# The last three attention units and the routing of the last five token tiles, written out by hand

## The chip, the cores and the metric

One NeuronCore of one Trainium2 chip runs one program. The metric is the device time of one execution in microseconds (us), as the median of several runs. The engines are TensorE (PE, its weight loads PEld), VectorE (DVE), ScalarE (ACT), GpSimd (POOL) and SyncE (SP, which issues most DMAs).

## The reference, cut to what matters

```python
x = _attn_ref(q, k, v)          # 2 x 8 heads, 576 tokens, head size 64; heads 0-3 local mask (32), 4-7 strided mask
x = x.transpose(0, 2, 1, 3).reshape(1152, 512)
x = _moe_ref(x, w_gate, w1, w2, capacity)     # top-1 of 8 experts
return _moe2_ref(x, w_in, w_out, a, b)        # rational activation between two products

# _moe_ref
logits = x @ w_gate
expert_idx = np.argmax(logits, axis=1)
gate_w = softmax(logits)[np.arange(N), expert_idx]
# token i takes the next place of its expert, if there is one below capacity
h = np.maximum(np.einsum('ecd,edf->ecf', disp, w1), 0.0)
y = np.einsum('ecf,efd->ecd', h, w2)
out[i] = gate_w[i] * y[expert_idx[i], pos[i]]  # 0 for tokens without a place
```

All arithmetic is float32 in effect; the products of the expert stage are float32 matmuls.

## The kernel before, in words

The program has three stages. The first is attention, in 16 units (u0 to u15). A unit is one batch, one pair of heads and half of their query blocks. Each unit passes through steps that a software pipeline spreads over four turns of a loop: `stage_a` (scores on PE: a mask product and then queries by keys), `stage_exp` (row maximum on DVE, exponentials on ACT), `stage_norm` (sum and reciprocal on DVE, then the scaling of the two heads' weights, both halves on POOL), `stage_b` (transposes on PE into a PSUM tile `tp` for each head), `stage_copy` (`tp` to `pT`, head 0 on DVE for these units and head 1 on ACT), `stage_c` (weights by values on PE, into `pv`) and `stage_evac` (`pv` into the 512 x 1152 array `xT` on DVE). Units 12 to 15 fill the first two of xT's four rows of 128 features for the second batch; a unit covers 288 tokens.

The routing needs, for each tile of 128 tokens (nine tiles, 0 to 8): `gate_mm`, the logits, from four products (d = 0 to 3, one for each 128 features); `gate_arg`, nine small DVE steps and one on ACT that find the expert and the gate weight; `rows_mm` and `put_rows`, which transpose the tile's rows back, scale them by the gate and write them to the DRAM array `xd`; `rank_mm` and `rank_post`, which count each token's place in its expert and build one-hot rows `ohr` on DVE; and `index_mm`, which turns the one-hots into token numbers. `places` sorts the experts by their count, `index` writes the lists `idx` for the gathers (128 entries and up to 64 more for each expert), `ordi` is the order of the experts (SP needs it to load their weights), and `over` computes `flag`, which says whether any expert needs the long way round.

In the loop the tiles 0 to 3 are routed in turns 9 to 15, out of a list `dq` of small steps; `hook(14, rank(0, 4))` puts the ranking of tiles 0 to 3 into turn 14. Three extra turns (`LE = 3`) then drain the pipeline: no new unit starts, and gates, rows and ranks of tiles 4 and 5 are put between the last steps. Tiles 6 to 8 follow behind the loop.

Each engine takes its instructions in the order in which the program lists them, so the order written here is the order on each engine. All waits between engines are semaphores.

Then the memory pools of attention are closed and those of the second stage opened over the same memory. `gather(0)` issues two indirect DMAs on POOL (expert 0's 192 rows out of `xd`), `warm(16)` runs 16 dummy matmuls on PE, SP starts two weight loads, all engines read `flag` and take the branch over the long way, `warm(12)` runs 12 more dummy matmuls, and `xpose(0)` transposes the gathered rows. The expert stage follows: eight experts, each four weight tiles of the first product (line 912 of the profile) and four of the second (line 927); weights stream in on SP. The third stage is the dense product with the rational activation.

The lines that the steps below speak of: 325 and 329 scores, 352 to 355 softmax, 363 to 366 normalising, 375 transposes, 383 copies, 393 values, 401 into xT, 423 logits, 457 rows, 463 and 465 scaled rows, 480 and 483 rank, 494 one-hots, 513 index products, 551 to 554 index lists, 697 gathers, 281 dummy matmuls, 712 and 713 transposes of the gathered rows, 854 and 855 flag and branch.

Of the kernel before, what the change touches and what calls it, by code (L numbers as in the profile page):

```python
# [19 lines left out]
T = B * S  # L20
# [18 lines left out]
NL = 64  # L39
DUM2 = (16, 12)  # L40
LE = 3
# [98 lines left out]
def build(tc, qt, kt, vv, masks, cb, cf, wl, cap, wf, ab, out):  # L140
# [227 lines left out]
    def stage_b(u):  # L368
        s_ = st[u]
        nb, Q, KN = geom(*u[1:])[:3]  # L370
        s_["tp"] = []
        for h in range(2):
# [3 lines left out]
            s_["tp"].append(tp)  # L376

    def stage_copy(u, h):
        s_ = st[u]
        nb, Q, KN = geom(*u[1:])[:3]  # L380
        if h == 0:
            s_["pT"] = att.tile([128, 2, 3, 128], F32, name="pT", bufs=2)[0:KN, :, 0:nb, 0:Q]
        (A.copy if h or u[1:] in ((2, 1), (3, 1)) else V.tensor_copy)(out=s_["pT"][:, h], in_=s_["tp"][h])

# [132 lines left out]
    kc, key, pos, wide, offe = (rt.tile([128, E], F32, name=x) for x in ("kc", "key", "pos", "wide", "offe"))  # L517
    gtm, pm, m8 = (rt.tile([128, E, E], F32, name=x) for x in ("gtm", "pm", "m8"))
    ordi = rt.tile([128, E], I32, name="ordi")

    def bc(x, axis, n=E):
        return x.unsqueeze(axis).to_broadcast([128, n, E] if axis == 1 else [128, E, n])

    def places(total):

        return [
            lambda: V.tensor_scalar(out=kc, in0=total, scalar1=capf, scalar2=None, op0=ALU.min),
            lambda: V.scalar_tensor_tensor(out=key, in0=kc, scalar=float(E), in1=cft[:, F_PRIO:F_PRIO + E], op0=ALU.mult, op1=ALU.add),
            lambda: V.tensor_tensor(out=gtm, in0=bc(key, 1), in1=bc(key, 2), op=ALU.is_gt),
            lambda: V.tensor_reduce(out=pos, in_=gtm, axis=AX.X, op=ALU.add),  # L530
            lambda: V.tensor_tensor(out=pm, in0=bc(cft[:, F_IOTA:F_IOTA + E], 2), in1=bc(pos, 1), op=ALU.is_equal),
        ]
# [6 lines left out]
    def by_expert(out, x):  # L539

        V.tensor_tensor(out=m8, in0=pm.rearrange("p s e -> p e s"), in1=bc(x, 1), op=ALU.mult)
        V.tensor_reduce(out=out, in_=m8, axis=AX.X, op=ALU.add)

    def index():

        ip = late()[0][:, 0:4 * E].rearrange("p (h a e) -> p h a e", h=2, a=2)
        im = att.tile([128, 2, E, 2 * E], F32, name="im", bufs=1)
        ib = att.tile([128, 2, E], F32, name="ib", bufs=1)
        idx = rt.tile([128, 2, E], I32, name="idx")
        for h in range(2):  # L550
            V.tensor_tensor(out=im[:, h].rearrange("p s (a e) -> p s a e", a=2), in0=pm.unsqueeze(2).to_broadcast([128, E, 2, E]),
                            in1=ip[:, h].unsqueeze(1).to_broadcast([128, E, 2, E]), op=ALU.mult)
            V.tensor_reduce(out=ib[:, h], in_=im[:, h], axis=AX.X, op=ALU.add)
            V.tensor_scalar(out=idx[:, h], in0=ib[:, h], scalar1=capm[:, h:h + 1], scalar2=float(T), op0=ALU.mult, op1=ALU.add)
        by_place(ordi, cft[:, F_IOTA:F_IOTA + E])
        return idx
# [61 lines left out]
    for i, t in ((11, 0), (12, 1), (13, 2), (14, 3)):  # L618
        hook(i, lambda t=t: row(t))
    hook(14, lambda: rank(0, 4))  # L620
    for i in range(n + LE):
        ua, uc, un, ub = (at(units, i - k) for k in (0, 3, 1, 2))
        if uc:
            stage_copy(uc, 0)
            stage_copy(uc, 1)
        if ua:
            stage_a(ua)
            stage_exp(ua)
        if uc:
            stage_c(uc)  # L630
        if i == n:
            dq.extend([lambda: gate_mm(6, 9, (2, 3), late()[1]), lambda: index_mm(0, 4)])
        if i == n + 1:
            gates(4, 6)
            row(4)
            rank(4, 6)
            row(5)
        if i == n + 2:
            gate_mm(6, 9, (0,), late()[1])
        for f in hooks.pop(i, []):  # L640
            f()
        if un:
            stage_norm(un)
        if i >= n and ub:
            stage_b(ub)
        if i >= n and uc:
            stage_evac(uc)
        dv(2)
        if i < n and ub:
            stage_b(ub)  # L650
        if i < n and uc:
            stage_evac(uc)
        dv(5 if i < n + 2 else 0)
# [64 lines left out]
    idc = rt.tile([128, NT], I32, name="idc")  # L718
    flag = rt.tile([128, 1], I32, name="flag")

    def over():

        by_place(cnt[:, 4:], kc)
        V.tensor_tensor(out=key, in0=cnt[:, 4:], in1=cft[:, F_SEL:F_END], op=ALU.is_gt)
        V.tensor_reduce(out=flag, in_=key, axis=AX.X, op=ALU.max)

# [358 lines left out]
```

## Time and profile before

| | |
|---|---|
| median of 3 runs | 464.94 us (464.47 to 466.04) |
| the profiled execution | 466.55 us, of which the span from first to last instruction is 464.8 us |
| PE busy | 431.6 us, 93% of the span |
| DVE busy | 325.7 us, 70% |
| ACT busy | 241.7 us, 52% |
| POOL busy | 54.9 us, 12% |
| mean granted TensorE clock | 0.952 of full speed |

Full speed is 2.4 GHz; 0.50 in the profile is the lower of the clock's two levels, 1.2 GHz. The attention stage runs from the start to about 65 us, its tail and the routing to about 103 us, the experts from there to about 245 us and the dense product to the end. The profile is one execution, 1.6 us above the median of the runs, so differences are taken within it and then set against the median.

### The profile page before, as it was taken

To read this page: it belongs to the slowest core of one execution; us is meant where nothing else is said; L and a number is where in the kernel's file an instruction comes from. 1 tells how busy PE (TensorE), PEld (TensorE's weight loads), DVE (VectorE), ACT (ScalarE), POOL (GpSimd) and SP (SyncE) were. 2 spreads that over 40 slices of the span, in tenths; PEclk is the share of its full clock that TensorE was granted. 3 is DMA by queue.
4 is the path that set the end of the run, shared out by engine and by line. 5 is a ranking of instruction groups with operands and counts; after the bars stand their busy time and mean duration, and the time that the engine had idled before them with its cause. 6 is when DMAs were issued, how large, how long until landed. Compare 5 with 4: busy or idle time off the path is not lost.

```text
span 464.8 us, 7758 instructions
## 1 busy us (share of the span) xinstructions
PE 431.6 (93%) x2778; PEld 389.4 (84%) x2779; DVE 325.7 (70%) x720; ACT 241.7 (52%) x579; POOL 54.9 (12%) x86
## 2 busy tenths in 40 slices
PE   7899768769999999999999979999989999999994
PEld 4667557649999999999999969988879989899973
DVE  2786642613466554565676999999979999969992
ACT  3785730202031221212224877878868888678881
POOL 3454430110101011010000000000020000110002
PEclk9999985659999999999999989999999999999998
DMA  8999660339975767878784000000010000010001
GB/s 294 341 357 356 221 233 2 114 129 381 417 299 173 261 212 222 258 236 285 268 291 147 1 1 0 1 0 0 2 68 1 0 1 1 23 47 1 1 1 68
DMA packets 20986, 66.42 MB, mean 143 GB/s; under 512 B 2824, under 2 KB 3208, under 8 KB 20944
## 3 DMA queue, kind: packets, MB, share of 16 engines
q1 hardware_dynamic: 19312, 60.96, 37.2%
q0 software_dynamic: 1632, 4.93, 3.3%
q8 instruction: 23, 0.38, 0.3%
q14 instruction: 19, 0.16, 0.1%
HBM read 61.16 MB, written 4.72 MB: 142 GB/s over the span
## 4 chain that ended last, share of the span: by engine, by line
PE 49%; DVE 22%; issue 4%; ACT 2%; POOL 0%; POOLq 0%
PE bank L912 15%; PE bank L927 14%; DVE p L1013 4%; DVE q L1012 3%; PE bank L1039 3%; DVE glo L1020 3%; PE bank L1037 3%; PE bank L1038 3%; PE bank L969 3%; DVE q L1011 3%; PE bank L970 3%; PE bank L971 3%; DVE q L999 3%; DVE p L1001 3%; PE bank L712 2%
## 5 line engine op out<-in xcount | busy, mean ns | idle before, releaser
L912 PE MATMUL bank<-x,wraw 128*128 128x192 f32 (+7 forms) x512 | 71.5, 302 | 0.0
L927 PE MATMUL bank<-h,wraw 128*128 128x192 f32 (+7 forms) x512 | 71.5, 299 | 0.0
L912 PEld LDWEIGHTS bank<-x,wraw 128*128 128x128 f32 x512 | 70.6, 194 | 0.1
L927 PEld LDWEIGHTS bank<-h,wraw 128*128 128x128 f32 x512 | 69.1, 191 | 0.2
L969 PE MATMUL bank<-yh,whi 128*128 128x384 f32 x192 | 64.9, 338 | 1.3 <-ACT ob L1043 1.3
L970 PE MATMUL bank<-yl,whi 128*128 128x384 f32 x192 | 64.8, 338 | 0.1
L971 PE MATMUL bank<-yh,wlo 128*128 128x384 f32 x192 | 64.7, 337 | 0.0
L1039 PE MATMUL bank<-whi,glo 128*128 128x512 f32 x144 | 58.0, 403 | 2.7 <-DVE glo L1020 2.7
L1037 PE MATMUL bank<-whi,ghi 128*128 128x512 f32 x144 | 57.5, 399 | 0.5 <-ACT ghi L1019 0.5
L1038 PE MATMUL bank<-wlo,ghi 128*128 128x512 f32 x144 | 57.2, 397 | 0.0
L913 ACT ACTIVATE h<-bank 128x384 f32<-128x384 f32 (+7 forms) x32 | 13.8, 432 | 77.8 <-PE bank L912 77.8
L1009 ACT ACTIVATE r<-q,qb 128x384 f32<-128x384 f32 x48 | 29.6, 617 | 25.6 <-DVE q L999 25.6
L355 ACT ACTIVATE pt<-sc,nb 96x128 f32<-96x128 f32 (+1 forms) x88 | 30.8, 370 | 16.9 <-DVE nb L353 15.9
L969 PEld LDWEIGHTS bank<-yh,whi 128*128 128x128 f32 x192 | 36.2, 189 | 3.4 <-ACT ob L1043 1.7
L970 PEld LDWEIGHTS bank<-yl,whi 128*128 128x128 f32 x192 | 36.1, 188 | 2.1 <-DVE yl L885 0.4
L239 DVE TENSOR_TENSOR wlo<-wcv,whi 128x1024 fp32r<-128x1024 f32 x16 | 19.6, 1223 | 25.6 <-ACT whi L227 24.5
L1045 POOL DMA_INDIRECT out_dram<-ob,idc x9 | 8.8, 977 | 233.7 <-ACT ob L1043 231.2
L1039 PEld LDWEIGHTS bank<-whi,glo 128*128 128x128 f32 x144 | 27.4, 191 | 10.7 <-DVE glo L1020 4.4
L971 PEld LDWEIGHTS bank<-yh,wlo 128*128 128x128 f32 x192 | 36.1, 188 | 0.0
L998 ACT ACTIVATE q<-ah,babs 128x384 f32<-128x384 f32 x48 | 34.1, 711 | 1.6
L1037 PEld LDWEIGHTS bank<-whi,ghi 128*128 128x128 f32 x144 | 27.4, 190 | 5.6 <-ACT ghi L1019 0.8
L1000 ACT ACTIVATE p<-bank,nab 128x384 f32<-128x384 f32 x48 | 31.4, 653 | 0.0
(157 smaller groups left out, 714.3 us busy)
## 6 DMA issues: line engine op xcount, KB each, us to landing
wraw<-in_wl_dram SPq DMA_DIRECT2D x64, 512.0 KB, 5.3
wraw<-in_wf_dram SPq DMA_DIRECT2D x32, 512.0 KB, 5.8
vt<-in_vv_dram SPq DMA_DIRECT2D x8, 384.0 KB, 5.5
qz<-in_qt_dram SPq DMA_DIRECT2D x8, 288.0 KB, 6.2
kz<-in_kt_dram SPq DMA_DIRECT2D x8, 288.0 KB, 8.3
xd<-xr SPq DMA_DIRECT2D x9, 256.0 KB, 2.0
xg<-xd,idx POOLq DMA_INDIRECT x15, 4.7
mkt<-in_masks_dram SPq DMA_DIRECT2D x1, 160.0 KB
```

The source lines that it names most:

```text
L355: A.activation(out=s_["pt"][:, h, i], in_=s_["sv"][h][:, i], func=AF.Exp, bias=bias[:, i:i + 1], scale=0.125, accum_out=s_["sm"][:, h, i:i ...
L912: PE.matmul(hp[:, i], lhsT=w[:, d, 128 * i:128 * i + 128], rhs=x2[:, d], start=(d == 0), stop=(d == 3), skip_group_check=True)
L927: PE.matmul(o, lhsT=w[:, f], rhs=h2[:, f], start=(f == 0), stop=(f == 7), skip_group_check=True)
L969: PE.matmul(hp, lhsT=wh, rhs=yh[:, d], start=(d == 0), stop=False)
L970: PE.matmul(hp, lhsT=wh, rhs=yl[:, d], start=False, stop=False)
L971: PE.matmul(hp, lhsT=wl, rhs=yh[:, d], start=False, stop=(d == 3))
L998: A.activation(out=q, in_=ah, func=AF.Identity, scale=babs[:, 1:2], bias=babs[:, 0:1])
L1000: A.activation(out=p1, in_=hp, func=AF.Identity, scale=nab[:, 3:4], bias=nab[:, 2:3])
L1009: A.activation(out=r0, in_=q, func=AF.Abs_reciprocal_sqrt, bias=qb)
L1037: PE.matmul(o, lhsT=ghi[:, ts], rhs=wh, start=(f == 0), stop=False)
L1038: PE.matmul(o, lhsT=ghi[:, ts], rhs=wl, start=False, stop=False)
L1039: PE.matmul(o, lhsT=glo[:, ts], rhs=wh, start=False, stop=(f == NF - 1))
```

## The change

The loop ends after 16 turns; the three draining turns are replaced by a list of steps written out. Logits of tiles 4 to 8 go into one PSUM tile, product by product as their features become ready. The ranking of tiles 0 to 3 moves from turn 14 to the middle of that list. The second half of `stage_norm` of u14 and u15 goes from POOL to DVE. The copies of u14 and u15 are both on ACT. Tiles 4 to 8 are ranked together, not as 4 and 5 and then 6 to 8. The index lists are two tiles, and `over` and `ordi` stand between their two halves. There is one block of 20 dummy matmuls ahead of the branch and none behind it. Early weight loads go out a few turns sooner, and `xr` has five buffers in place of three.

```diff
-DUM2 = (16, 12)
+DUM2 = (20,)
...
-    def stage_norm(u):
+    def stage_norm(u, second=G):
...
-        for h in range(2):
-            G.tensor_tensor(out=pt[:, h], in0=pt[:, h], in1=rs[:, h].unsqueeze(2).to_broadcast([Q, nb, KN]), op=ALU.mult)
+        for h, eng in enumerate((G, second)):
+            eng.tensor_tensor(out=pt[:, h], in0=pt[:, h], in1=rs[:, h].unsqueeze(2).to_broadcast([Q, nb, KN]), op=ALU.mult)
...
-        xr = att.tile([128, DM], F32, name="xr", bufs=3)
+        xr = att.tile([128, DM], F32, name="xr", bufs=5)
...
-        idx = rt.tile([128, 2, E], I32, name="idx")
+        idx = [rt.tile([128, E], I32, name=f"idx{h}") for h in range(2)]
         for h in range(2):
+            if h:
+                over()
+                by_place(ordi, cft[:, F_IOTA:F_IOTA + E])
...
-        by_place(ordi, cft[:, F_IOTA:F_IOTA + E])
...
-    for i in range(2, 17):
-        hook(i, lambda i=i: pump(min(2 * NEARLY - loads[0], 1 if i < 9 else 2)))
+    for i in range(2, n):
+        hook(i, lambda i=i: pump(min(2 * NEARLY - loads[0], 1 if i < 7 else 2)))
...
-    hook(14, lambda: rank(0, 4))
-    for i in range(n + LE):
+    for i in range(n):
...
+    u13, u14, u15 = units[-3:]
+    ip, lp = late()
+    PE.matmul(lp[:, 0:5 * NL].rearrange("p (t e) -> p t e", e=NL), lhsT=wz, rhs=wz[:, 0:NL].unsqueeze(1).to_broadcast([128, 5, NL]),
+              start=True, stop=False, skip_group_check=True)
+    logits((4, 5, 6), (2, 3))
+    logits((4, 5), (0,))
+    stage_copy(u13, 0)
+    stage_copy(u13, 1)
+    stage_c(u13)
+    stage_norm(u15, V)
+    stage_b(u14, (1, 0))
+    stage_evac(u13)
+    stage_copy(u14, 1)
+    stage_copy(u14, 0, A.copy)
+    logits((4, 5), (1,))
+    first = gate_arg(4, 6, lp)
+    stage_c(u14)
+    stage_b(u15, (1, 0))
+    run(first[:3])
+    stage_evac(u14)
+    stage_copy(u15, 1)
+    stage_copy(u15, 0, A.copy)
+    logits((7, 8), (2, 3))
+    rk0 = rank_mm(0, 4)
+    stage_c(u15)
+    run(first[3:])
+    stage_evac(u15)
+    logits((6, 7, 8), (0,))
+    post0 = rank_post(0, 4, rk0)
+    run(post0[-1:] + post0[:-1])
+    logits((6, 7, 8), (1,))
...
+    rows_mm(4, gps[0])
+    put_rows(4, gps[0])
+    rows_mm(5, gps[1])
+    put_rows(5, gps[1])
+    second = gate_arg(6, 9, lp[:, 2 * NL:])
+    run(second[:6])
+    rk = rank_mm(4, 9)
+    for t in (6, 7, 8):
+        rows_mm(t, gps[t - 4])
+    run(second[6:])
+    index_mm(0, 4)
+    post = rank_post(4, 9, rk)
+    put_rows(6, gps[2])
+    put_rows(8, gps[4])
+    run(post[:2])
+    put_rows(7, gps[3], V)
+    run(post[2:-1])
     index_mm(4, 9)
-    for f in places(rk[:, 3]):
-        f()
+    run(places(rk[:, 5]))
     idx = index()
...
     warm(DUM2[0])
     pump(2)
-    over()
...
-    warm(DUM2[1])
     xpose(0)
```

On PE, behind u13's transposes (the first row of each piece), the order before is this; `sc` and `ms` are PSUM tiles, `ohr` the one-hots:

```order
L375 MATMUL tp<-cft,pt 128x96 x6
L393 MATMUL pv<-pT,vt 64x96 x6
L375 MATMUL tp<-cft,pt 128x96 x6
L418 LDWEIGHTS wz
L418 MATMUL sc_1078<-wz 128x192
L423 MATMUL sc_1078<-cft,xT 128x64 x6
L510 LDWEIGHTS wz
L510 MATMUL sc_1077<-wz 128x32
```

and now it is this:

```order
L375 MATMUL tp<-cft,pt 128x96 x6
L665 LDWEIGHTS wz
L665 MATMUL sc_1042<-wz 128x320
L654 MATMUL sc_1042<-cft,xT 128x64 x8
L393 MATMUL pv<-pT,vt 64x96 x6
L375 MATMUL tp<-cft,pt 128x96 x6
L654 MATMUL sc_1042<-cft,xT 128x64 x2
L393 MATMUL pv<-pT,vt 64x96 x6
L375 MATMUL tp<-cft,pt 128x96 x6
L654 MATMUL sc_1042<-cft,xT 128x64 x4
```

Eight logit products (line 654 of the changed kernel) have moved ahead of u13's values product (line 393), into the place where PE before went straight to it; further logits stand between the later steps.

On DVE, at the end of the routing, the order before is this (the index lists are written at line 554, `flag` at 725):

```order
L554 TENSOR_SCALAR idx<-ib,capm 128x8
L551 TENSOR_TENSOR im<-pm,sc_1077 128x128
L553 TENSOR_REDUCE ib<-im 128x8
L554 TENSOR_SCALAR idx<-ib,capm 128x8
L536 TENSOR_TENSOR m_128<-pm,cft 128x64
L537 TENSOR_REDUCE ordi<-m_128 128x8
L536 TENSOR_TENSOR m_128<-pm,kc 128x64
L537 TENSOR_REDUCE cnt<-m_128 128x8
L724 TENSOR_TENSOR key<-cnt,cft 128x8
L725 TENSOR_REDUCE flag<-key 128x1
```

and now it is this:

```order
L564 TENSOR_SCALAR idx_1250<-ib,capm 128x8
L537 TENSOR_TENSOR m_126<-pm,kc 128x64
L538 TENSOR_REDUCE cnt<-m_126 128x8
L548 TENSOR_TENSOR key<-cnt,cft 128x8
L549 TENSOR_REDUCE flag<-key 128x1
L537 TENSOR_TENSOR m_126<-pm,cft 128x64
L538 TENSOR_REDUCE ordi<-m_126 128x8
L561 TENSOR_TENSOR im<-pm,sc_1041 128x128
L563 TENSOR_REDUCE ib<-im 128x8
L564 TENSOR_SCALAR idx_1251<-ib,capm 128x8
```

The six operations for `flag` and `ordi` have moved from behind the second half of the index to between its halves.

## Rows read from the trace of the kernel before

**Rows 1.** Costliest groups: busy us, mean ns | idle of the engine before them.
```profile
L912 PE MATMUL bank<-x,wraw 128*128 128x192 f32 (+7 forms) x512 | 71.5, 302 | 0.0
```
**Rows 2.** Busy time of each engine by stretch, granted clock, DMA share, GB/s.
```profile
62.00:64.00 2.00, 0.00 (x0) 0.00 (x0) 1.97 (x7) 1.65 (x10) 1.61 (x2) 1.00 0.92 350
64.00:66.00 2.00, 1.38 (x17) 1.26 (x18) 1.30 (x7) 0.00 (x0) 0.89 (x2) 0.85 0.92 358
66.00:68.00 2.00, 2.00 (x12) 1.99 (x11) 0.45 (x1) 0.40 (x1) 0.72 (x1) 0.50 0.23 92
...
84.00:86.00 2.00, 2.00 (x19) 1.94 (x18) 0.90 (x6) 0.91 (x3) 0.41 (x2) 0.53 0.64 240
...
104.00:106.00 2.00, 2.00 (x8) 2.00 (x7) 0.90 (x5) 0.00 (x0) 1.05 (x2) 0.50 0.57 184
106.00:108.00 2.00, 2.00 (x13) 2.00 (x12) 0.51 (x2) 0.49 (x1) 0.00 (x0) 0.91 1.00 375
```
**Rows 3.** Timeline of PE from 57 us: start, duration, what [idle before <- who ended it].
```profile
56.68 0.66 PE L457 MATMUL ms<-cft,xT 128*128 128x128 f32 x4
57.17 0.66 PE L375 MATMUL tp<-cft,pt 96*128 96x96 f32 x6
58.76 0.18 PE L480 MATMUL ms<-oh,cbt 128*128 128x32 bf16 x1 [0.93 <-ACT xr L463]
...
60.77 0.71 PE L375 MATMUL tp<-cft,pt 96*128 96x96 f32 x6
64.62 0.72 PE L393 MATMUL pv<-pT,vt 128*64 128x96 f32 x12 [3.14 <-DVE pT L383]
```
**Rows 4.** Line 423, 42 to 45 us and 72 to 75.7 us: ns min/median/max, first, last.
```profile
L423 PE MATMUL ms<-cft,xT x16: 274/275/324, 42.7 to 44.4; 128*128 128x64 f32 x16
...
L423 PE MATMUL ms<-cft,xT x16: 368/421/422, 72.1 to 75.3; 128*128 128x64 f32 x16
```
**Rows 5.** Timeline of DVE, one-hots of tiles 0 to 3 and end of routing.
```profile
62.57 1.64 DVE L494 TENSOR_SCALAR ohr<-cbt,r 128x192 bf16<-128x192 bf16 x4
...
86.53 0.74 DVE L465 TENSOR_SCALAR xr<-sc,gate 128x512 f32<-128x512 f32 x1
...
89.66 0.23 DVE L554 TENSOR_SCALAR idx<-ib,capm 128x8 int32<-128x8 f32 x1
...
90.44 0.23 DVE L554 TENSOR_SCALAR idx<-ib,capm 128x8 int32<-128x8 f32 x1
...
91.80 0.16 DVE L725 TENSOR_REDUCE flag<-key 128x1 int32<-128x8 f32 x1
```
**Rows 6.** Durations (ns) of one-hots beside POOL, of POOL's scaling, of a DVE product.
```profile
L494 DVE TENSOR_SCALAR ohr<-cbt,r x4: 257/374/864, 62.6 to 63.9; 128x192 bf16<-128x192 bf16 x4
...
L366 POOL TENSOR_TENSOR pt<-pt,rs 96x384 f32<-96x384 f32 x8 | 6.4, 824 | 8.5 <-PE tp L375 5.6 <-DVE rs L364 1.5 <-PE pv L393 1.4
...
L999 DVE TENSOR_TENSOR q<-q,ah x48: 548/550/559, 255.5 to 450.6; 128x384 f32<-128x384 f32 x48
```
**Rows 7.** The branch on PE's queue, ns.
```profile
L855 PEldq COMPARE_BRANCH  x1: 5452/5452/5452, 92.6 to 92.6; - x1
```
**Rows 8.** Timeline from the gathers to the first expert.
```profile
91.74 1.17 POOL L697 DMA_INDIRECT xg<-xd,idx  x1 [6.74 <-DVE cnt L537]
...
93.22 0.90 POOL L697 DMA_INDIRECT xg<-xd,idx  x1 [0.31 <-remote]
...
98.36 2.72 PE L281 MATMUL bank<-wz 128*128 128x256 bf16 x12 [4.56 <-PEq L855]
...
100.88 2.05 PE L712 MATMUL bank<-cft,xg 128*128 128x128 f32 x8
...
102.86 12.36 PE L912 MATMUL bank<-x,wraw 128*128 128x192 f32 x64
```
**Rows 9.** Gathers of line 697, issue to landing: 91 to 95 us, 103 to 106 us.
```profile
DMA to landing us min/median/max: 7.4/7.4/7.4
...
DMA to landing us min/median/max: 4.7/5.3/5.8
```

More of the change, by code (lines that the diff above doesn't have):

```diff
@@ L364, in stage_norm, with stage_b @@
         V.reciprocal(out=rs, in_=sm)
-        for h in range(2):
-            G.tensor_tensor(out=pt[:, h], in0=pt[:, h], in1=rs[:, h].unsqueeze(2).to_broadcast([Q, nb, KN]), op=ALU.mult)
-    def stage_b(u):
+        for h, eng in enumerate((G, second)):
+            eng.tensor_tensor(out=pt[:, h], in0=pt[:, h], in1=rs[:, h].unsqueeze(2).to_broadcast([Q, nb, KN]), op=ALU.mult)
+    def stage_b(u, hs=range(2)):
         s_ = st[u]
         nb, Q, KN = geom(*u[1:])[:3]
-        s_["tp"] = []
-        for h in range(2):
+        s_.setdefault("tp", {})
+        for h in hs:
             tp = psa.tile([128, 512], F32, name="tp", bufs=2)[0:KN, 0:nb * Q].rearrange("p (n q) -> p n q", n=nb)
@@ L375, in stage_b, with stage_copy @@
                 PE.transpose(tp[:, i], s_["pt"][:, h, i], idf[0:Q, 0:Q])
-            s_["tp"].append(tp)
-    def stage_copy(u, h):
+            s_["tp"][h] = tp
+    def stage_copy(u, h, eng=None):
         s_ = st[u]
         nb, Q, KN = geom(*u[1:])[:3]
-        if h == 0:
+        if "pT" not in s_:
             s_["pT"] = att.tile([128, 2, 3, 128], F32, name="pT", bufs=2)[0:KN, :, 0:nb, 0:Q]
-        (A.copy if h or u[1:] in ((2, 1), (3, 1)) else V.tensor_copy)(out=s_["pT"][:, h], in_=s_["tp"][h])
+        (eng or (A.copy if h or u[1:] in ((2, 1), (3, 1)) else V.tensor_copy))(out=s_["pT"][:, h], in_=s_["tp"][h])
     def stage_c(u):
@@ L517, in build @@
     kc, key, pos, wide, offe = (rt.tile([128, E], F32, name=x) for x in ("kc", "key", "pos", "wide", "offe"))
-    gtm, pm, m8 = (rt.tile([128, E, E], F32, name=x) for x in ("gtm", "pm", "m8"))
+    m8, pm = (rt.tile([128, E, E], F32, name=x) for x in ("m8", "pm"))
     ordi = rt.tile([128, E], I32, name="ordi")
+    flag = rt.tile([128, 1], I32, name="flag")
     def bc(x, axis, n=E):
@@ L542, in by_expert, with over @@
         V.tensor_reduce(out=out, in_=m8, axis=AX.X, op=ALU.add)
+    def over():
+        by_place(cnt[:, 4:], kc)
+        V.tensor_tensor(out=key, in0=cnt[:, 4:], in1=cft[:, F_SEL:F_END], op=ALU.is_gt)
+        V.tensor_reduce(out=flag, in_=key, axis=AX.X, op=ALU.max)
     def index():
@@ L553, in index @@
             V.tensor_reduce(out=ib[:, h], in_=im[:, h], axis=AX.X, op=ALU.add)
-            V.tensor_scalar(out=idx[:, h], in0=ib[:, h], scalar1=capm[:, h:h + 1], scalar2=float(T), op0=ALU.mult, op1=ALU.add)
-        by_place(ordi, cft[:, F_IOTA:F_IOTA + E])
+            V.tensor_scalar(out=idx[h], in0=ib[:, h], scalar1=capm[:, h:h + 1], scalar2=float(T), op0=ALU.mult, op1=ALU.add)
         return idx
@@ L625, in build @@
             stage_copy(uc, 1)
-        if ua:
-            stage_a(ua)
-            stage_exp(ua)
+        stage_a(ua)
+        stage_exp(ua)
         if uc:
             stage_c(uc)
[L631 to L639, printed above, removed]
         for f in hooks.pop(i, []):
@@ L642, in build @@
         if un:
-            stage_norm(un)
-        if i >= n and ub:
+            stage_norm(un, G if i < n - 1 else V)
+        dv(2)
+        if ub:
             stage_b(ub)
-        if i >= n and uc:
+        if uc:
             stage_evac(uc)
[L648 to L653, printed above, removed]
-    assert not hooks, hooks
-    free[:] = ["tp", "ms"]
-    lp = late()[1]
-    gate_mm(6, 9, (1,), lp)
+        dv(5)
@@ L658, in build, with logits, run @@
+    assert not hooks, hooks
+    def logits(ts, ds):
+        for t in ts:
+            for d in ds:
+                PE.matmul(lp[:, NL * (t - 4):NL * (t - 3)], lhsT=xT[:, d, 128 * t:128 * t + 128],
+                          rhs=cft[:, F_WG + E * d:F_WG + E * d + NL], start=False, stop=(d == 1), skip_group_check=True)
+    def run(fs):
+        for f in fs:
+            f()
     while dq:
         dv()
-    last = gate_arg(6, 9, lp)
-    for f in last[:6]:
-        f()
-    gps = [*(psa.tile([128, 512], F32, name=f"sc{h}", bufs=2) for h in range(2)), psa.tile([128, 512], F32, name="pv")]
@@ new lines, in build @@
+    stage_c(u15)
[5 more added lines that the diff above has]
+    logits((6, 7, 8), (1,))
+    gps = [*(psa.tile([128, 512], F32, name=f"sc{h}", bufs=2) for h in range(2)), *(psa.tile([128, 512], F32, name="tp", bufs=2) for _ in range(2)),
+           psa.tile([128, 512], F32, name="pv")]
+    rows_mm(4, gps[0])
[3 more added lines that the diff above has]
+    second = gate_arg(6, 9, lp[:, 2 * NL:])
@@ L718, in build @@
     idc = rt.tile([128, NT], I32, name="idc")
[L719 to L725, printed above, removed]
     def offsets():
```

22 lines of the change are left out of this document (4 added, 18 removed).

## The prediction

> **What bounds the kernel now.** I read the costliest groups first. They show that in the expert stage PE waits for nothing: the 512 matmuls of line 912 have no idle time ahead of them [rows 1]. So whatever moves the first expert matmul moves everything behind it by as much, and the question is when that matmul starts (102.86 us [rows 8]) and at which clock. Then I read the busy time by stretch around the end of attention. From 62 to 64 us PE does nothing at all while DVE is full; then the granted clock falls from 1.00 to 0.50 and is still at 0.53 from 84 to 86 us, though PE is busy again [rows 2]. The timeline says what PE waited for: u13's values product starts at 64.62 after 3.14 us of idling for DVE's copy of `pT` [rows 3], and that copy stood on DVE behind the four one-hots of tiles 0 to 3, which took 1.64 us [rows 5]. From there to the index PE works through logits, rows and ranks at 1.2 GHz: 16 records of logits start within 1.7 us at the full clock and within 3.2 us at the lower one [rows 4]. Last, I read the part from the gathers to the first expert: two gathers at 91.74 and 93.22, PE held in its branch, 12 dummy matmuls, transposes of the gathered rows at 100.88, and the first expert matmul at 102.86 [rows 8].
>
> I use three marks of the trace before: A, the end of the first half of the index, 89.66 + 0.23 = 89.89 [rows 5]; X, the first transposition of gathered rows, 100.88; E, the first expert matmul, 102.86 [rows 8]. X is A + 10.99 and E is X + 1.98.
>
> **Part 1, the ranking leaves the place ahead of u15's scores.** Before, PE stood 0.93 us at the ranking of tiles 0 to 3 for ACT, with u15's scores queued behind it [rows 3]. u12's transposes end at 57.17 + 0.66 = 57.83; u15's scores can start there, 0.93 earlier. u13's transposes, which ended at 60.77 + 0.71 = 61.48, then end near 60.5.
>
> **Part 2, the tail of attention.** From 60.5 PE has, up to the rows of tile 7: 40 records of logits (20 products, two records each) at 1.7/15 = 0.113 us, 4.5 us; three values products and two sets of transposes at about 0.72 [rows 3], 3.6 us; four sets of rows at 0.66 [rows 3], 2.6 us; the two ranks, at about 0.4 each (the old one's 0.18 is one of its four matmuls [rows 3]), 0.8 us. That is 11.5 us at the full clock. Consecutive pieces overlap by 0.1 to 0.2 us (57.17 lies 0.17 ahead of the end of the piece at 56.68 [rows 3]); for some 11 pieces I take off 1.3. Waits are added: for u12's and u13's move into `xT` (0.5), for ACT's two copies of u14 (0.3), and for the choice of the expert of tiles 6 to 8, six small DVE steps of about 0.2 that only partly hide behind the rows of tiles 4 and 5 (1.2). So the rows of tile 7 are ready at 60.5 + 11.5 - 1.3 + 2.0 = 72.7, and DVE scales them there. Before, that scaling started at 86.53 [rows 5], 3.36 us ahead of A. The changed program has five one-hots between them, not three: 2 x 0.26 more [rows 6]. A comes to 72.7 + 3.36 + 0.52 = 76.6, which is 13.3 us earlier. I allow 1.0 for handovers that I have not listed: **-12.3**, bounds -13.3 and -10.6.
>
> The sum holds if the clock stays at 1.00, and for that I look at what PE did before it fell: nothing, from 61.48 to 64.62 [rows 3]. In the new order that stretch holds 12 records of logits that wait for nothing, four more that wait for u12's features, u13's values and u14's transposes; the longest wait that I find is below 0.8 us. The one-hots that held the copy are now behind u15.
>
> The lower bound takes in the split of the normalising. Each half took POOL 0.82 us, and a DVE product of that size takes 0.55 [rows 6]; side by side a unit would be ready after 0.82 in place of 1.64. But one of the four one-hots that ran beside POOL took 864 ns where the quickest took 257 [rows 6], so the two engines do hold each other up. The row is of another operation (one tensor and a scalar); whether the float32 product is held too, no row shows, so it costs 0.55 or up to 0.55 + 0.82 for each of two units, and the moves into `xT` queue behind it. I take half of it as hidden, since u14's transposes are due only after u13's values product; the bound of -10.6 has all of it, 2 x 0.82 = 1.6, on top of the 1.0 for handovers.
>
> The Trainium skill, in "SBUF — State Buffer", section "SBUF: two separate sides", says that DVE and GpSimd share one pair of SBUF ports as an exclusive lock, which a DVE operation with two SBUF inputs needs as well. By it this product would be held for the whole of POOL's instruction, or hold it, and the unit would be ready after 0.55 + 0.82 = 1.37; taken by the rows alone it lies between 0.82 and 1.64. By that rule the sum would come out 0.5 to 1.1 later than by the other end, which is inside the bounds.
>
> **Part 3, the index and the gathers.** The first gather does not start earlier relative to A. In the built program its wait on DVE is for the last write of the second index half, as before, because the gathered tile lies over memory that attention frees. And that second half now ends later: the six operations that stood behind it took from 90.44 + 0.23 = 90.67 to 91.80 + 0.16 = 91.96 [rows 5], 1.29 us, and are now ahead of it. So the second gather starts at A + (93.22 - 89.89) + 1.29 = A + 4.62 [rows 8]. A gather lands 7.4 us after its issue in the trace of before, where it shares the queues with two weight loads, and after 4.7 to 5.8 elsewhere [rows 9]. The weight loads now come ahead of the gathers (SP waits for `ordi` alone), so I take 5.3: X = A + 9.9, bounds A + 9.3 and A + 12.0. That X can follow the landing at all is the removal of the 12 dummy matmuls (2.72 us [rows 8]), which before ended at 101.08, after the landing at 93.22 + 7.4 = 100.6 at the latest. PE's branch took 5.45 us from 92.6 [rows 7], to A + 8.2. The flag is ready 1.3 us sooner but PE reaches the branch behind 20 dummy matmuls whose first waits for the second half's read of PSUM, so it starts at A + 2.8 to A + 4.2 and ends by A + 9.7: below the gather. Change of X - A: **-1.1**, bounds -1.7 and +1.0.
>
> **Part 4, the clock at the first expert.** Before, it was 0.50 up to about 106.4 (0.91 over 106 to 108 [rows 2]), 3.5 us into the expert stage and 8.0 us after PE had begun with the 12 dummies. Now nothing precedes the transposes. If the clock rises 3.5 us after E the term is 0; if 8.0 us after PE begins, E runs at half for 6.0 us, 2.5 more, of which half is lost: 1.25. I take **+0.6**, bounds 0 and +1.7.
>
> The earlier weight loads and the two more `xr` buffers I cost at nothing: the DMA queues are at 0.92 up to 66 us and then at 0.23 [rows 2], while the loads that they fill are not used before the expert stage; if an attention input came late behind them, a unit would wait.
>
> **Sum.** -12.3 - 1.1 + 0.6 = -12.8. From the profiled execution's 466.55 that is 453.75; from the median of 464.94, which is 1.6 lower, it is 452.1. I say **452.5**.
>
> **Rivals.** *The clock falls all the same*, near 65 us, because the logits keep PE less at work than they look: for it speaks that the clock did not rise for 20 us in which PE was busy with just these logits [rows 2, 4]; against it, that it fell only behind an empty stretch. Then the work after 65 us (about 22 records of logits at 0.1 more each, two values products and two sets of transposes at 0.4 to 0.5 more, four sets of rows at 0.4 more) takes some 5.8 us longer: -7.0, **458**. *The order makes a new wait of some 2 us* (DVE held by POOL, gathers landing after 7.4 us as before): -9 to -10, **455.5**. *Slower:* the clock stays at 0.50 deep into the expert stage, with no dummies ahead of it. Expert matmuls then take twice as long, 0.5 us lost for each us, so from 25 us at the lower clock on the gain is gone; 40 us would give **472**. For it speaks only the 20 us of before at 0.50 with PE busy; against it, that the same expert matmuls raised it 3.5 us after they began. *No change*: if the first expert waited for weights rather than for the gather, E would not move; but between 62 and 102 us the weight loads are issued behind `ordi`, which moves with A.
>
> **How the numbers follow.** Forecast 0.60 (own range 449.5 to 455), a new wait 0.15, the clock falls 0.18, no change 0.03, slower 0.04. Leaving 2 in 10 out, the range runs from 449.0 (the good bounds of all terms give -15.0, and the runs spread by 1.6) to 458.5, which takes in the new wait and half of the fallen clock. A measurement of this kernel tells 0.3% from nothing, 1.4 us. Faster 0.93, within it 0.03, slower 0.04.
>
> **What would show it.** Right: PE without a gap of over 1 us from 58 to 72 us and the clock at 1.00 throughout; DVE's scaling of tile 7 near 73 to 74; the second gather 1.3 us later relative to the first half of the index; X at the gather's landing and no longer behind dummies. Wrong: the clock at 0.50 at 66 to 70 us; X later than A + 11; the clock at 0.50 for more than 7 us after E; PE waiting at line 912.

## The result, and the profile after

The changed kernel takes **450.45 us** (median of 4 runs, 449.76 to 450.8); the kernel before, in the same rounds, 464.71. The ratio is 0.9686, 95% interval 0.9663 to 0.9709. Forecast were 452.5 us and a range of 449.0 to 458.5. The profiled execution took 450.65 us with a span of 448.4, against 466.55 and 464.8 before. One execution of e2 and two of e7 below lie more than 1.5% above the fastest of their kernel and count as slow; the ratios leave them out, the medians do not.

First the stretches that answer to [rows 2]: busy time by stretch, then granted clock, DMA share, GB/s.

```profile
60.00:62.00 2.00, 2.00 (x27) 1.88 (x26) 1.79 (x7) 1.28 (x7) 0.20 (x1) 1.00 0.87 311
62.00:64.00 2.00, 2.00 (x23) 1.70 (x23) 1.86 (x7) 1.19 (x7) 1.33 (x2) 1.00 0.71 268
64.00:66.00 2.00, 1.97 (x24) 1.62 (x25) 1.01 (x5) 0.88 (x3) 0.67 (x1) 1.00 0.01 4
66.00:68.00 2.00, 2.00 (x30) 1.94 (x29) 1.29 (x7) 0.93 (x4) 0.39 (x2) 1.00 0.00 0
...
74.00:76.00 2.00, 0.92 (x8) 0.70 (x7) 1.69 (x9) 0.20 (x1) 0.00 (x0) 1.00 0.93 342
76.00:78.00 2.00, 0.34 (x2) 0.28 (x3) 1.79 (x10) 0.00 (x0) 0.00 (x0) 0.70 0.02 8
...
88.00:90.00 2.00, 2.00 (x8) 1.90 (x7) 1.49 (x8) 0.00 (x0) 1.25 (x2) 0.50 0.05 10
90.00:92.00 2.00, 2.00 (x13) 2.00 (x12) 0.22 (x1) 0.00 (x0) 0.59 (x1) 0.88 1.00 295
```

From 62 to 64 us PE was empty before [rows 2]; now it is full. The clock stays at 1.00 until the routing itself leaves PE without work: the index products end at 74.92 us, the next matmul starts at 77.66, and the clock falls between 76 and 78 us. PE's timeline answers to [rows 3] and, from 77 us, to [rows 8]:

```profile
58.00 0.66 PE L375 MATMUL tp<-cft,pt 96*128 96x96 f32 x6
...
60.52 0.71 PE L375 MATMUL tp<-cft,pt 96*128 96x96 f32 x6
61.08 0.30 PE L665 MATMUL sc<-wz 128*128 128x320 bf16 x1
61.22 2.08 PE L654 MATMUL sc<-cft,xT 128*128 128x64 f32 x16
63.23 0.73 PE L393 MATMUL pv<-pT,vt 128*64 128x96 f32 x12
63.89 0.71 PE L375 MATMUL tp<-cft,pt 96*128 96x96 f32 x6
...
77.66 4.42 PE L281 MATMUL bank<-wz 128*128 128x256 bf16 x20 [2.74 <-DVE im L561]
86.09 2.08 PE L747 MATMUL bank<-cft,xg 128*128 128x128 f32 x8 [4.00 <-DMA xg<-xd,idx]
88.10 11.81 PE L938 MATMUL bank<-x,wraw 128*128 128x192 f32 x64
99.75 5.36 PE L953 MATMUL bank<-h,wraw 128*128 128x192 f32 x32
```

u13's transposes (60.52) are now followed by 16 records of logits, and u13's values start behind those without a noted wait. DVE's timeline answers to [rows 5]:

```profile
72.42 0.75 DVE L465 TENSOR_SCALAR xr<-tp,gate 128x512 f32<-128x512 f32 x1
...
75.92 0.23 DVE L564 TENSOR_SCALAR idx<-ib,capm 128x8 int32<-128x8 f32 x1
76.77 0.16 DVE L549 TENSOR_REDUCE flag<-key 128x1 int32<-128x8 f32 x1
...
77.87 0.23 DVE L564 TENSOR_SCALAR idx<-ib,capm 128x8 int32<-128x8 f32 x1
```

POOL's answers to the gathers of [rows 8]:

```profile
79.17 1.17 POOL L732 DMA_INDIRECT xg<-xd,idx  x1 [7.69 <-DVEq L882]
80.65 0.90 POOL L732 DMA_INDIRECT xg<-xd,idx  x1 [0.31 <-remote]
```

Their landing, of line 732 from 70 to 86 us, to [rows 9]:

```profile
DMA to landing us min/median/max: 5.4/6.1/6.7
```

And the branch on PE's queue to [rows 7]:

```profile
L882 PEldq COMPARE_BRANCH  x1: 353/353/353, 78.7 to 78.7; - x1
```

So A = 75.92 + 0.23 = 76.15, X = 86.09 and E = 88.10: 13.74, 14.79 and 14.76 us earlier than before.

### The profile page after: what moved, and what is told of

The parts are those of the page before. It is cut to its first block, busy times and chain, and to the rows that moved or that the text cites. A ratio compares the mean times of both kernels' runs of the same rounds, so it can differ in the third digit from the quotient of the medians.

```text
span 448.4 us, 7728 instructions
## 1 busy us (share of the span) xinstructions
PE 422.3 (94%) x2764; PEld 380.2 (85%) x2765; DVE 324.7 (72%) x718; ACT 242.8 (54%) x580; POOL 53.9 (12%) x84
## 4 chain that ended last, share of the span: by engine, by line
PE 61%; DVE 13%; issue 3%; ACT 2%; DMA 1%; POOL 0%; POOLq 0%
PE bank L938 16%; PE bank L953 14%; PE bank L1065 5%; PE bank L1063 5%; PE bank L1064 5%; PE bank L995 5%; PE bank L996 5%; PE bank L997 5%; DVE p L1039 2%; PE bank L747 2%; DVE q L1038 2%; DVE q L1037 2%; DVE q L1025 2%; DVE glo L1046 2%; DVE p L1027 2%
```

## The experiments

Two more marks help to compare profiles whose early part differs: **U**, the start of u13's transposes (60.77 before, 60.52 after), and **F**, the first matmul of the experts' second product (line 953 after, 99.75). The table takes them from the timeline of one execution of each kernel. Ratios are against the kernel before in the same rounds. The medians are not: in the rounds of e1, e2, e3 and e7 the kernel before took 464.82 us, in those of e4, e5, e6 and e8 464.17, in those of e9 to e12 465.88, so versions from different rounds are compared by their ratios.

| run | median us | ratio (95%) | A - U | E - A | F - A |
|---|---|---|---|---|---|
| before | 464.71 | 1 | 29.12 | 12.97 | 25.17 |
| after | 450.45 | 0.9686 (0.9663 to 0.9709) | 15.63 | 11.95 | 23.60 |
| e1, before, one block of dummies | 464.21 | 0.9986 (0.9969 to 1.0004) | 28.36 | 11.50 | 23.36 |
| e2, before, ranking late | 462.72 | 0.9917 (0.9877 to 0.9957) | 29.12 | 12.90 | 24.30 |
| e11, before, gap filled | 459.38 | 0.9859 (0.9825 to 0.9892) | 23.76 | 12.66 | 25.21 |
| e3, after, ranking early | 452.83 | 0.9772 (0.9716 to 0.9829) | 16.41 | 12.28 | 24.47 |
| e7, after, logits behind | 458.09 | none given | 22.84 | 12.27 | 24.51 |
| e6, after, norm on POOL | 450.66 | 0.9693 (0.9667 to 0.9719) | 15.62 | 12.19 | 24.70 |
| e4, after, flag last | 449.29 | 0.9677 (0.9647 to 0.9707) | 15.63 | 11.32 | 23.71 |
| e5, after, 17 dummies more | 449.41 | 0.9664 (0.9632 to 0.9695) | 15.62 | 12.89 | 23.96 |
| e8, after, early gather | 450.66 | 0.9693 (0.9665 to 0.9721) | 16.84 | 11.03 | 23.44 |
| e9, after, three buffers | 451.38 | 0.9697 (0.9666 to 0.9728) | 16.84 | 12.33 | 24.40 |
| e12, early gather, four buffers | 450.10 | 0.9670 (0.9637 to 0.9703) | 16.13 | 11.21 | 24.12 |
| e10, e12 with flag last | 450.09 | 0.9663 (0.9633 to 0.9693) | 16.13 | 11.02 | 23.83 |

**Is it the empty stretch that drops the clock?** Run e11 fills it and changes nothing else:

```diff
+        if i == n:
+            wps = psa.tile([128, 512], F32, name="sc0", bufs=2)
+            for _ in range(28):
+                PE.matmul(wps[:, 0:256]..., lhsT=wz, rhs=wz..., start=True, stop=True)
         if uc:
             stage_c(uc)
```

> The kernel before with 28 dummy matmuls on PE ahead of u13's values product, that is in the 3.1 us in which it did nothing; they write to a score bank that is free, and nothing else is changed. Theory one (the clock fell because PE stood, not because of what came behind): the clock stays at 1.00 past 65.4 us, up to the next long wait for the copy of pT at 75.7 or for good; u13's values product starts where it did (64.6) and the first half of the index ends 3 to 7 us earlier: 458 to 461.5 us. Theory two (the work behind the gap, logits of 64 columns, lets the clock fall whatever stands ahead): the clock is at 0.50 within a few us of 65.4 and the time is that of the kernel before, 463.5 to 465.

PE's timeline in that run:

```profile
60.20 3.22 PE L632 MATMUL sc<-wz 128*128 128x256 bf16 x28
63.50 0.72 PE L393 MATMUL pv<-pT,vt 128*64 128x96 f32 x12
...
64.79 1.48 PE L423 MATMUL sc<-cft,xT 128*128 128x64 f32 x12
```

Its busy time by stretch, columns as above:

```profile
64.00:66.00 2.00, 2.00 (x25) 1.88 (x22) 0.84 (x2) 0.40 (x1) 1.59 (x2) 1.00 0.32 127
66.00:68.00 2.00, 2.00 (x28) 1.73 (x28) 0.25 (x1) 0.00 (x0) 0.00 (x0) 1.00 0.04 10
68.00:70.00 2.00, 2.00 (x21) 1.96 (x18) 0.20 (x1) 0.00 (x0) 0.00 (x0) 1.00 0.00 0
70.00:72.00 2.00, 0.24 (x4) 0.17 (x5) 1.41 (x7) 0.50 (x2) 0.39 (x2) 1.00 0.00 0
72.00:74.00 2.00, 2.00 (x21) 1.88 (x20) 0.87 (x4) 0.00 (x0) 0.00 (x0) 0.74 0.00 0
```

Theory one holds. u13's values start as far behind U as before (3.85 us), so no wait has gone; the same 12 records of logits take 1.48 us where they took 2.72 before, and the clock falls only behind the next empty stretch, the 1.76 us ahead of u15's values. A - U is 5.36 us shorter, and the median 6.5 us lower (5.0 to 8.2 by the interval), with work that computes nothing.

**Which half of the change keeps it full?** Two things could: the one-hots leave DVE's queue ahead of the copy, and the logits fill PE. e2 does the first without the second, e3 the second without the first, e7 takes the second out of the changed kernel.

```diff
e2 (to before)
-    hook(14, lambda: rank(0, 4))
...
-            dq.extend([lambda: gate_mm(6, 9, (2, 3), late()[1]), lambda: index_mm(0, 4)])
+            dq.extend([lambda: gate_mm(6, 9, (2, 3), late()[1])])
...
             gates(4, 6)
+            rank(0, 4)
+            dq.append(lambda: index_mm(0, 4))
e3 (to after)
+    hook(14, lambda: rank(0, 4))
...
-    rk0 = rank_mm(0, 4)
-    post0 = rank_post(0, 4, rk0)
-    run(post0[-1:] + post0[:-1])
e7 (to after)
-    logits((4, 5, 6), (2, 3))
-    logits((4, 5), (0,))
     stage_copy(u13, 0)
...
     stage_b(u14, (1, 0))
+    logits((4, 5, 6), (2, 3))
+    logits((4, 5), (0,))
     stage_evac(u13)
```

> The kernel before with the ranking of tiles 0 to 3 (its matmuls, its four one-hots and the index product) moved from turn 14 to the second drain turn, ahead of the rows of tile 4; nothing else of the change. Theory one (the one-hots in DVE's queue ahead of the copy of pT emptied PE, and that dropped the clock): u13's values product starts near 62, the clock stays at 1.00 from 62 to 76 us for the most part, and the first half of the index ends 6 to 11 us earlier; 454 to 459 us. Theory two (the old order leaves PE too little to do whatever DVE does, the logits must be put there): PE has a gap of over 1.5 us between 60 and 66 all the same, the clock falls to 0.50 there, and only 1 to 2 us are gained; 463 us.

> The changed kernel with the ranking of tiles 0 to 3 put back into turn 14, ahead of u15's scores and with its one-hots ahead of the copy of pT; the logits still fill PE behind u13's transposes. Theory one (the place of the one-hots was what mattered): PE stands again for 1.5 us or more between 60 and 65, the clock falls to 0.50 there, the first half of the index ends some 7 us later; 456 to 459 us. Theory two (the logits that wait for nothing are what holds the clock, wherever the one-hots stand): the gaps are below 1.2 us, the clock stays at 1.00 up to 75 us, the index ends 0.3 to 1.5 us later; 450.8 to 452 us.

> The changed kernel with the 16 records of logits (tiles 4 to 6, features 2 and 3, and tiles 4 and 5, feature 0) behind u14's transposes in place of ahead of u13's values product. PE then has nothing behind u13's transposes until DVE has copied pT: an empty stretch of about 1.0 to 2.2 us near 61. Theory one (an empty stretch of that size drops the clock): the clock is at 0.50 from about 64 us for 10 us or more, and the first half of the index ends 6 to 8 us later than 76.15; 456 to 458.5 us. Theory two (the copy is early now that the one-hots are gone, the clock holds): the index ends 0.3 to 1.5 us later and the time is 450.8 to 452 us.

PE's timeline of e2 at u13's values:

```profile
61.06 0.38 PE L393 MATMUL pv<-pT,vt 128*64 128x96 f32 x2 [1.14 <-DVE pT L383]
61.93 0.71 PE L393 MATMUL pv<-pT,vt 128*64 128x96 f32 x10 [0.49 <-ACT pT L383]
```

The same place in e3:

```profile
64.02 0.66 PE L655 MATMUL sc<-cft,xT 128*128 128x64 f32 x4 [0.42 <-DVE xT L401]
65.11 0.72 PE L393 MATMUL pv<-pT,vt 128*64 128x96 f32 x12 [0.42 <-DVE pT L383]
```

And in e7:

```profile
61.96 0.95 PE L393 MATMUL pv<-pT,vt 128*64 128x96 f32 x12 [1.63 <-DVE pT L383]
62.84 0.71 PE L375 MATMUL tp<-cft,pt 96*128 96x96 f32 x6
63.39 2.98 PE L654 MATMUL sc<-cft,xT 128*128 128x64 f32 x16
```

In e2 theory two holds: the values start 2.0 us sooner behind U, but PE still stands 1.6 us in two pieces, the clock falls behind it (0.50 over 64 to 66 us), and A - U is 29.12 as before. In e3 the one-hots hold the copy again, yet the logits run meanwhile: two waits of 0.42, the clock at 1.00 to 78 us, A 1.72 later than after (0.78 in A - U, and 0.94 ahead of U where the ranking waits for ACT again). That is theory two, at somewhat more than its 1.5 us. In e7 theory one holds: one wait of 1.63 is back, the clock is at 0.51 over 64 to 66, and A - U is 7.2 longer with the same instructions. So in the profiled executions the filling is what holds the clock; the one-hots' place shortens the stretch but does not close it.

The runs without a profile fit this only by their mean granted clock: e7's four runs are 457.71, 458.48 and 460.33 us at 0.953 to 0.960, and 451.65 at 0.982; e2's ten have three near 457.8 at 0.965 to 0.971 and the slower ones mostly at 0.942 to 0.954; one of e3's four is 458.27 at 0.961. So with the 1.63 us of standing that the profiles of e2 and e7 show, the clock seems to fall in most executions and not in all. e7's profiled execution, 457.71 us, is a safer figure than its median. The four of the changed kernel lie at 0.974 to 0.979.

**The split of the normalising** (e6: both halves on POOL).

```diff
-            stage_norm(un, G if i < n - 1 else V)
+            stage_norm(un)
...
-    stage_norm(u15, V)
+    stage_norm(u15)
```

> The changed kernel with both halves of the normalising of u14 and u15 on POOL, one behind the other, as before the change. A unit would be ready after 2 x 0.82 = 1.64 us in place of the 1.2 to 1.3 of the changed kernel (0.55 on DVE beside 1.10 on POOL). Theory one (hidden: u14's transposes stand behind u13's values, u15's behind u14's): the index ends within 0.3 us of 76.15 and the time is within 1 us of 450.45. Theory two (the split shortens a wait): u14's or u15's transposes start 0.4 to 1 us later, and the index with them; 450.9 to 452, or more if the clock falls with it.

u14's half on DVE in the changed kernel, from DVE's timeline:

```profile
61.66 0.55 DVE L366 TENSOR_TENSOR pt<-pt,rs 96x384 f32<-96x384 f32 x1
```

Its other half on POOL:

```profile
61.80 1.10 POOL L366 TENSOR_TENSOR pt<-pt,rs 96x384 f32<-96x384 f32 x1 [2.49 <-DVE rs L364]
```

Both halves on POOL in e6:

```profile
62.11 1.61 POOL L366 TENSOR_TENSOR pt<-pt,rs 96x384 f32<-96x384 f32 x2 [2.48 <-DVE rs L364]
```

Theory one holds: A - U is 15.62 against 15.63. The split makes a unit ready after 62.90 - 61.66 = 1.24 in place of 1.61 us, and nobody waits for it.

**The dummies, and what stands ahead of the first expert** (e1, e5).

```diff
e1 (to before)
-DUM2 = (16, 12)
+DUM2 = (20,)
...
-    warm(DUM2[1])
e5 (to after)
-DUM2 = (20,)
+DUM2 = (20, 17)
...
+    warm(DUM2[1])
     xpose(0)
```

> The kernel before with one block of 20 dummy matmuls ahead of the branch and none behind it, as the change has it. My theory (this part of the change is worth little): the first half of the index ends where it did, at 89.9 us; the first transposition of gathered rows no longer stands behind dummies that end at 101.1 and starts at the gather's landing, 98.6 to 100.6; against that the clock may rise up to 1.25 us later. Time -1.5 to +1.0 us against the kernel before, 463.2 to 465.7. Rival (the dummies ahead of the experts are what decides the clock there): the clock stays at 0.50 for 6 us or more behind the first expert matmul, and the kernel is slower by 1 us or more, 466. Rival (the dummies were the main cost): faster by 2.5 us or more, 462.

> The changed kernel with 17 more dummy matmuls behind the branch, in the 4 us in which PE waits for the gathered rows. They take 17 x 0.21 = 3.6 us at the lower clock and end near 85.7, ahead of the landing at 86.1. Theory one (PE at work up to the transpositions brings the clock up sooner): the clock is at 1.00 by the first expert matmul or before, the transpositions take 1.0 in place of 2.0 us and the 2.4 us of expert matmuls at the lower clock cost 1.2 less; 1 to 2.2 us faster, 448.2 to 449.4. Theory two (dummies do not move the clock's rise): 450 to 451. Theory three (the dummies end behind the landing): X 0.3 to 1 us later, and what the clock gives back is lost again.

PE's timeline of e1 from the dummies on:

```profile
90.32 4.01 PE L281 MATMUL bank<-wz 128*128 128x256 bf16 x20 [1.93 <-DVE im L551]
99.37 2.18 PE L712 MATMUL bank<-cft,xg 128*128 128x128 f32 x8 [5.04 <-DMA xg<-xd,idx]
```

The same of e5:

```profile
76.28 4.42 PE L281 MATMUL bank<-wz 128*128 128x256 bf16 x20 [2.74 <-DVE im L561]
83.10 2.88 PE L281 MATMUL bank<-wz 128*128 128x256 bf16 x17 [2.39 <-issue]
85.78 1.96 PE L747 MATMUL bank<-cft,xg 128*128 128x128 f32 x8
87.67 11.24 PE L939 MATMUL bank<-x,wraw 128*128 128x192 f32 x64
```

e1: the gathered rows are transposed when they land, 9.39 us behind A in place of 10.99; in the median 0.6 us, which the interval does not tell from nothing. e5: theory three, with the clock of theory one. The second block comes 2.39 us late behind the branch, the dummies push X to A + 11.0, and the 64 expert matmuls (11.24 against 11.81) give 0.6 of that back, since the clock is up when they start. The time is that of the changed kernel within the intervals.

e5's busy time by stretch shows what became of the clock between the two blocks:

```profile
80.00:82.00 2.00, 0.71 (x4) 0.26 (x3) 0.00 (x0) 0.00 (x0) 0.16 (x1) 0.83 0.96 367
82.00:84.00 2.00, 0.90 (x9) 0.81 (x9) 0.00 (x0) 0.00 (x0) 0.00 (x0) 1.00 0.22 66
84.00:86.00 2.00, 2.00 (x13) 1.52 (x10) 0.00 (x0) 0.00 (x0) 0.00 (x0) 0.52 0.02 6
86.00:88.00 2.00, 2.00 (x10) 1.16 (x10) 0.07 (x1) 0.48 (x1) 0.00 (x0) 0.63 0.04 8
```

The first block had brought the clock to 1.00; behind the 2.39 us of standing it was at 0.50 again. In eight of the ten profiles of the changed kernel and its variants the 20 dummies raise it in this way, and in all eight it falls again ahead of the first expert matmul; in that of the changed kernel itself, and in e4's, it does not rise there at all.

**The start of the gathers and the buffers** (e4, e8, e9, e12, e10).

```diff
e4 (to after)
             if h:
-                over()
-                by_place(ordi, cft[:, F_IOTA:F_IOTA + E])
...
+        by_place(ordi, cft[:, F_IOTA:F_IOTA + E])
+        over()
         return idx
e8 (to after; e12 has xr bufs=4, e10 also e4's edit)
-        xr = att.tile([128, DM], F32, name="xr", bufs=5)
+        xr = att.tile([128, DM], F32, name="xr", bufs=3)
...
-        g = ex.tile([128, 2, DM], F32, name="xg", bufs=1)
+        g = [(ex if h else rt).tile([128, DM], F32, name=f"xg{h}", bufs=1) for h in range(2)]
... (g[0:n, h] becomes g[h][0:n] in the gather and in the transposes)
e9 (to after)
-        xr = att.tile([128, DM], F32, name="xr", bufs=5)
+        xr = att.tile([128, DM], F32, name="xr", bufs=3)
```

> The changed kernel with the order by place and the flag behind both halves of the index, as before the change (the clock, the ranks and the dummies as changed). The second half ends 1.29 us earlier, so the gathers start that much earlier, while the weight loads wait for the order and the branch for the flag as before. Theory one (what the gathers gain in start they lose in landing, because the weight loads now go with them): they land after 6.5 to 7.4 us, where the changed kernel has 5.4 to 6.7; the first transposition starts 9.3 to 10.7 us behind the first half; time -0.6 to +0.8 us against the changed kernel's 450.45. PE's branch takes about 5.4 us again, as before, but ends ahead of the landing. Theory two (the start of the gathers sets the time): X is 1.3 us earlier, 449.1. Theory three (the branch becomes the last thing to be ready): X at the branch's end, later than 86.5.

> The changed kernel with the first 128 gathered rows in memory of their own, so that the first gather waits for the first half of the index and not for the last write of the second (and three buffers of xr in place of five, to make room). The first gather can be issued some 1.3 to 1.9 us earlier, the second behind it, once the second half is there. Theory one (the start of the gathers sets X): X 0.8 to 1.6 us earlier; 448.9 to 449.7. Theory two (the weight loads, issued at the same time, take the queues, or a wait for stored rows takes over): X within 0.4 us of where it was; 450 to 451. Theory three (the three buffers make the last rows wait for stores): the index ends later, and the time is above 451.

> The changed kernel with three buffers of xr in place of five, nothing else. In the run with the early gather, which had three too, DVE's scaling of tile 7 waited 1.21 us for a store of rows, and the first half of the index came 1.2 us later relative to u13's transposes. Theory one (that wait is the buffers' alone): the same 1.2 us here, 451.6. Theory two (the wait there came from the moved memory of the gathered rows): no wait, 450.4.

> The run with the early gather, but with four buffers of xr in place of three (five as changed). Theory one (the early gather gains 0.9 us at the first expert matmul, as seen before, and the fourth buffer takes away the 1.21 us wait for the store): the index ends at the same distance behind u13's transposes as in the changed kernel, the first expert matmul 0.9 us sooner; 449.3 to 449.9. Theory two (four buffers still wait): 450.4 or more.

> The changed kernel with the first 128 gathered rows in memory of their own, four buffers of xr, and the order and the flag behind both halves of the index. The first gather starts at about A + 1.2, the second at A + 2.1 to A + 2.8 (A + 4.5 as changed). Theory one (each 1 us that a gather starts sooner is worth at least half): the first transposition at A + 8.0 to A + 8.7, the first expert matmul at A + 10 to A + 11 (A + 11.95 as changed), and of that 0.5 to 0.8 goes to a clock that rises later behind it; 449 to 450. Theory two (the clock and the weight loads take all of it): 450.2 to 451.

DVE's timeline of e9 at the scaling of tile 7:

```profile
72.39 0.75 DVE L465 TENSOR_SCALAR xr<-tp,gate 128x512 f32<-128x512 f32 x1 [1.21 <-DMA xd<-xr]
```

The landing of the gathers in e4, of its gathers' line from 70 to 86 us:

```profile
DMA to landing us min/median/max: 6.5/6.8/7.2
```

PE's timeline of e12 from the landing on:

```profile
83.77 0.44 PE L747 MATMUL bank<-cft,xg 128*128 128x128 f32 x2 [2.55 <-DMA xg<-xd,idx]
85.08 1.49 PE L747 MATMUL bank<-cft,xg 64*128 64x64 f32 x6 [0.88 <-DMA xg<-xd,idx]
86.50 13.07 PE L938 MATMUL bank<-x,wraw 128*128 128x192 f32 x64
```

Three buffers cost 1.21 us in A - U (16.84), theory one of e9; four cost 0.50 (16.13): five rows' copies now lie close together. An earlier gather does bring E closer to A (from 11.95 to between 11.0 and 11.3), although in e4 it lands later behind its issue than after the change (6.5 to 7.2 against 5.4 to 6.7). In e8, whose X is 1.19 us closer to A, the three buffers' 1.21 takes that away again; in e12 the second gather lands late, and PE waits another 0.88 us for it. The 64 expert matmuls take 13.07 us in e12 against 11.81, since the clock is at 0.50 for 4.9 us behind E there, and 2.4 after the change. At F what is left lies within the spread: F - A is between 23.4 and 24.7 in all of the variants of the changed kernel, 23.4 to 24.1 in the four with an earlier gather and 23.6 to 24.7 in the others, one execution each. Whether the earlier start is worth anything in the time these runs do not tell: e4's median of 449.29 lies nearer to the theory that it is (449.1), e10's of 450.09 between its two. By the ratios (0.9677 and 0.9663) neither of them, nor any other version, beats the changed kernel (0.9686) by more than the intervals.

## Why the prediction held

The time came 2 us below the forecast and inside the range, and the mechanism, logits that keep PE at work and thereby the clock up, is the one that e11, e3 and e7 show. Two terms were mis-sized, both to the better side and both beyond their own bounds (parts 2 and 4).

**Part 1** was right: U lies 2.52 us behind u12's transposes, 3.60 before [rows 3], so 1.08 are gained (0.93 forecast).

**Part 2** had the right cause, and A came where the working said before the allowance (76.6 worked out, 76.15 measured). The 1.0 us "for handovers that I have not listed" was not needed: from the end of u13's transposes to the scaling of tile 7 it took 72.42 - 61.23 = 11.2 us, 12.2 forecast, waits included. The term is -13.74 against -12.3, beyond the good bound of -13.3. It would have been 0.8 larger still: u12's transposes start 0.83 later than in the profile of before. The clock was at 0.50 over 12 to 18 us in this execution, and at 1.00 in the one of before. e1, whose early program is that of before, shows the low clock there as well and has them at 58.02 too, so this is the execution and not the change. Of the 13.49 us by which A - U fell, e11 gains 5.36 by holding the clock alone, up to its second empty stretch; e7 shows that 7.2 of the 13.49 hang on where 16 records of logits stand; what is left for the order by itself no run separates. The prediction ascribed the full PE to both the logits and the departed one-hots; e2 and e3 show that the logits matter more.

The bounds for the normalising were needless, since nothing waited (e6). The Trainium skill, in "SBUF — State Buffer", section "SBUF: two separate sides", speaks of an exclusive lock between DVE and GpSimd. The trace agrees in part: POOL's half took 1.10 where it takes 0.80 in e6, DVE's half was not lengthened (0.55), and the unit was ready after 1.24, where that rule gives 1.37.

**Part 3** was right: second gather at A + 4.50 (A + 4.62 forecast; A + 3.33 before), X at A + 9.94 (9.9), behind the landing and not behind dummies, with landings of 5.4 to 6.7 us where 5.3 was taken. One step failed without harm: PE's branch was to take 5.45 us as before, and took 0.35.

**Part 4** is the term of the wrong sign: +0.6 forecast; the clock rose 2.4 us behind E (0.50 to 90, 0.88 over 90 to 92), not 3.5, which gives back 0.56, outside the bounds of 0 and +1.7. In twelve of the fourteen profiles the clock rises between 2.4 and 4.9 us behind E; in e2 and e5 it is up at E, although the rows were transposed at the lower clock there too. So the rise follows neither of the two rules that the prediction chose between, and one execution says little about this term.

**Two more buffers** were costed at nothing as a gain. That is right as a change of the time before, but the new order needs them: without them the index is 1.2 us later (e9).

**Sum.** -14.76 at E; -15.31 at F with the clock's 0.56; behind F the span is another 1.09 shorter. e1, e2 and e11, which have the old program from there on, are already 0.67 to 0.78 shorter there than the profile of before (span less F: 348.96 to 349.07 against 349.74), so most of that 1.09 belongs to the one execution of before. Of the 16.4 us in the span 15.9 arrive in the time, since the time is 2.25 us longer than the span in the changed kernel and 1.75 in the one before; no run shows why. The medians differ by 14.3: the profiled execution of before lies 1.8 above its median, that of after 0.2 above its own. That the time lies inside the range is in part luck: two terms missed to the same side, and at F the gain in the profile is already beyond the -15.0 of all good bounds together.

**The rivals**: the fallen clock was forecast at 458, 5.8 us on top; e7, which comes nearest to it, has 457.71 in the profiled execution, with A - U 7.2 longer, and of that 1.63 is the wait that the rival did not have. Its condition did not occur. What the prediction put in its favour was misread: PE was not busy for the 20 us in which the clock did not rise. It stood once more, for DVE's copy of u15, as PE's timeline of the kernel before shows:

```profile
77.46 1.23 PE L393 MATMUL pv<-pT,vt 128*64 128x96 f32 x12 [1.76 <-DVE pT L383]
```

The rival that forecast a slower kernel was added up too high: 3.5 us at the lower clock were paid before as well and 1.2 more stood in the forecast, so 40 us would give about 470 and not 472, and the gain would be gone at about 30 us, not 25. No wait of 2 us appeared, and the clock was up 2.4 us into the experts.

## What to carry to other kernels

Where TensorE stands for a copy on another engine and the granted clock falls behind that, the wait itself may be the smaller part of the price: find independent matmuls that can stand in front of the waiting one, and try dummies there first, since that shows in one run what the stretch costs. Moving the work that delays the copy may only shorten the stretch. A start that is won just ahead of a stretch at the lower clock has to be checked at a later mark, since a later rise can take it back.

## What was not expected

PE's branch took 5.1 to 5.5 us in the kernel before and in e1, e2 and e11, which are built on it, and 0.35 in the changed kernel and all its variants. Neither the second block of dummies (e1 lacks it, e5 has one) nor the order of the flag (e4 has the old one) decides it. The Trainium skill, in "Runtime: NRT & Kernel Launch", section "Instruction fetch mechanics", says that a taken branch whose target lies outside the instructions already held waits until they are fetched. That the long and the short times go with the two programs would fit; no run here moved the code alone, so the cause stays open. In the changed kernel the branch ends ahead of the gather's landing and sets nothing.
